# A GpSimd drain moved into the program's last tenth, two expert widths cut, and the last expert's tiles kept in order

## The chip, the cores and the metric

The kernel runs on one core of one Trainium2 chip. The metric is the device time of one execution in microseconds (us), as the median of several runs. A profile of one execution gives the trace from which the rows below are taken; its times count from the first instruction (the span's start). The engines are PE (matrix multiply; PEld is its weight load), DVE (vector), ACT (scalar), POOL (GpSimd, which also issues the indirect DMAs) and SP (which issues the plain DMAs). POOLq and the like are an engine's own instructions that are not computing, such as drains and branches.

## The reference

A windowed attention (4 batches, 8 heads, 576 positions of 64) is followed by a gated layer and by a mixture of 8 experts. The change is in the last part, which takes 2304 tokens `x` of 512 numbers:

```python
    expert_idx = np.argmax(logits, axis=1)
    ...
    gate_w = probs[np.arange(N), expert_idx]
    out = np.zeros((N, D), dtype=np.float32)
    for e in range(E):
        mask = expert_idx == e
        ...
        h = np.maximum(x[mask] @ w1[e], 0.0)
        out[mask] = gate_w[mask, None] * (h @ w2[e])
```

`w1[e]` is 512 by 1024, `w2[e]` 1024 by 512. The inputs send 346, 339, 358, 323, 280, 270, 222 and 166 tokens to the experts, in the order in which the kernel takes them.

## The kernel before

Each fp32 operand is split into a high and a low part, and every product is three matmuls (high by high, low by high, high by low). The experts are taken in slots: the first is expert 0, the second the fuller of the experts that are known first, the rest are in falling order of their token counts, which the kernel sorts at run time. Slot `e` has a static width, `CAPS[e]` (line 34): so many token columns are computed, and rows beyond the tokens that are there are not stored. Tokens beyond the width go to a loop behind the last expert (`tc.For_i`, line 1142), which runs as often as there are tiles left over; with the counts above it runs zero times, before and after the change.

The loop over the experts (lines 1091 to 1104) does for slot `e`:

- the gathers of the next expert's tokens, one indirect DMA on POOL for each tile of up to 128 rows (`gather`, line 928, tile `xg`), and the loads and splits of its weights (`weights`: 8 loads of 512 KB on SP, ACT's cast to `weh` at line 98, DVE's subtraction to `wel` at line 114);
- `ffn1`: eight groups `h0` to `h7`, each 12 matmuls (4 k-steps of 3) as wide as `CAPS[e]` (line 967), into one of two PSUM buffers; each group is evicted by ACT (relu, line 969) and then DVE (line 970);
- for each tile of the next expert the transposes `tx` (4 on PE, line 947), and for each own tile `ffn2`: 24 matmuls of 512 columns into `z` (line 983), DVE's scaling to `y` (line 987) and one indirect store on POOL (line 988). Each store to `out` waits for the landing of the one before.

These are the names of the code. In the rows the sixth expert is slot 5, the seventh slot 6 and the last slot 7; `h_2` is group 2, `xg_1`, `tx_1`, `y_1` and `z_1` belong to the second tile.

The order on each engine is not the code's: a scheduler that works on the whole program merges the steps. It issues z matmuls between h groups where it expects PE to wait. Each engine executes its own list in order. The code can pin an instruction with `tc.keep_in_program_order`, or tie what is inside a block behind an instruction with `tc.issue_after`; `latest(ENG.PE)[0]` is the last PE instruction written so far.

After the loop the program ends with a barrier: a drain on every engine (line 1203), on POOL three.

Of the kernel before, what the change touches and what calls it, by code (L numbers as in the profile page):

```python
# [1 line left out]

# [1 line left out]

# [21 lines left out]
E = 8  # L26
# [4 lines left out]
KD = DM // P  # L31
KF = FF // P
KE = FE // P
CAPS = [384, 384, 384, 352, 320, 320, 288, 256]
TCOL = NBLK
MAXOV = 16
BIG = 2.0 ** 42
# [21 lines left out]
def attn_ffn_moe(ctx: ExitStack, tc: tile.TileContext, qd, kd, vd, wgv, w_out, emb, tau, w1, w2, cst, ids, out):  # L59
    nc = tc.nc  # L60
# [13 lines left out]
    def pt(tag, name, bufs):  # L74
        return ps.tile([P, 512], F32, tag=tag, name=name, bufs=bufs)

    def row(name):
        return mid.tile([P, DM + 1], F32, tag="r", name=name)
# [487 lines left out]
    ENG = mybir.EngineType  # L566

    def latest(*engines):
        traced = nc.cur_bb.bb.instructions
        return [next(i for i in reversed(traced) if i.engine == e) for e in engines]  # L570
# [354 lines left out]
    def gather(e, t, idx, upto=None, w=P):  # L925
        x = row(f"xg{e}_{t}")
        if upto is None:
            nc.gpsimd.indirect_dma_start(out=x[0:w, :], out_offset=None, in_=x2_d, in_offset=IOA(ap=idx[0:w], axis=0))
        else:
            nc.gpsimd.memset(x, 0.0)  # L930
            nc.gpsimd.indirect_dma_start(out=x, out_offset=None, in_=x2_d[0:upto, :], in_offset=IOA(ap=idx, axis=0),
                                         bounds_check=upto - 1, oob_is_err=False)
        xg[e, t] = x
# [6 lines left out]
    def make_x(e, n, early=False):  # L940
        xe[e] = tuple(wide([P, KD, n], f"xe{z}_{e}", early) for z in range(2))

    def transp(e, t, u, w=P):
        xh, xl = xe[e]
        q = pt("t", f"tx{e}_{t}", 2)
        for k in range(KD):
            nc.tensor.transpose(q[:, k * P:k * P + w], xg[e, t][0:w, k * P:(k + 1) * P], ident[0:w, 0:w])
        qv = q.rearrange("p (k t) -> p k t", k=KD)[:, :, 0:w]
        sl = slice(u * P, u * P + w)
        hi_copy("a", xh[:, :, sl], qv)  # L950
        lo_sub("v", xl[:, :, sl], qv, xh[:, :, sl])

    def ffn1(e, n, early=False):
        xh, xl = xe.pop(e)
        hs = ([], [])
        for f in range(KE):
            if f % 4 == 0:
                for z in range(2):
                    hs[z].append(wide([P, 4, n], f"h{z}_{e}_{f}", early))
            hh, hl = (h[f // 4][:, f % 4, :] for h in hs)  # L960
            m = pt("s", f"h{e}_{f}", 2)
            cnt = 0
            fs = slice(f * P, (f + 1) * P)
            for k in range(KD):
                wh, wl = wset[e][k]
                for w, x in ((wh, xh), (wh, xl), (wl, xh)):
                    nc.tensor.matmul(m[:, :n], w[:, fs], x[:, k, :], start=(cnt == 0), stop=(cnt == 3 * KD - 1))  # L967
                    cnt += 1
            nc.scalar.activation(out=hh, in_=m[:, :n], func=AF.Relu)  # L969
            nc.vector.scalar_tensor_tensor(out=hl, in0=m[:, :n], scalar=0.0, in1=hh.bitcast(F32), op0=ALU.max,  # L970
                                           op1=ALU.subtract)
        return hs

    def ffn2(e, t, u, hs, idx, w=P):
        m = pt("m", f"z{e}_{t}", 3)
        cnt = 0
        ts = slice(u * P, u * P + w)
        for k in range(KE):
            hh, hl = (h[k // 4][:, k % 4, ts] for h in hs)
            wh, wl = wset[e][KD + k // 2]  # L980
            ds = slice((k % 2) * DM, (k % 2 + 1) * DM)
            for h, ww in ((hh, wh), (hl, wh), (hh, wl)):
                nc.tensor.matmul(m[0:w, :], h, ww[:, ds], start=(cnt == 0), stop=(cnt == 3 * KE - 1))  # L983
                cnt += 1
        x = xg.pop((e, t))
        y = row(f"y{e}_{t}")[:, 0:DM]
        nc.vector.tensor_scalar_mul(y[0:w, :], m[0:w, :], x[0:w, DM:DM + 1])  # L987
        nc.gpsimd.indirect_dma_start(out=out, out_offset=IOA(ap=idx[0:w], axis=0), in_=y[0:w, :], in_offset=None,  # L988
                                     bounds_check=NT - 1, oob_is_err=False)

    def ffn1_tok(e, t):
        xh, xl = xe.pop(e)
        hr = op_.tile([P, FE], F32, tag="c", name=f"hr{e}_{t}")
        hs = [op_.tile([P, KE, P], F32R, tag="c", name=f"hk{y}_{e}_{t}") for y in range(2)]
        for z in range(2):
            m = pt("s", f"ht{e}_{t}_{z}", 2)
            ds = slice(z * 512, (z + 1) * 512)
            cnt = 0
            for k in range(KD):
                wh, wl = wset[e][k]  # L1000
                for x, w in ((xh, wh), (xl, wh), (xh, wl)):
                    nc.tensor.matmul(m, x[:, k, :], w[:, ds], start=(cnt == 0), stop=(cnt == 3 * KD - 1))
                    cnt += 1
            nc.scalar.activation(out=hr[:, ds], in_=m, func=AF.Relu)
        for z in range(2):
            q = pt("t", f"th{e}_{t}_{z}", 2)
            for k in range(4):
                nc.tensor.transpose(q[:, k * P:(k + 1) * P], hr[:, (4 * z + k) * P:(4 * z + k + 1) * P], ident)
            qv = q.rearrange("p (k t) -> p k t", k=4)
            hi_copy("a", hs[0][:, 4 * z:4 * z + 4, :], qv)  # L1010
            lo_sub("v", hs[1][:, 4 * z:4 * z + 4, :], qv, hs[0][:, 4 * z:4 * z + 4, :])
        return [[h[:, 4 * z:4 * z + 4, :] for z in range(2)] for h in hs]
# [25 lines left out]
    def weights(e):  # L1038
        for j in range(NP):
            split_we(e, j, load_we(order[e], j, e), "a", "v")  # L1040

    hs = ffn1(0, CE * P)
# [8 lines left out]
    def load_col(e):  # L1051
        t0 = EARLY[e] if e < len(EARLY) else 0
        nt = -(-CAPS[e] // P) - t0
        cols[e] = cp.tile([P, nt], I32, tag=f"cols{e}", name=f"cols{e}")
        nc.sync.dma_start(cols[e], tab_v[:, bass.ds(order[e] * TCOL + t0, nt)])

    def col(e, t):
        t -= EARLY[e] if e < len(EARLY) else 0
        return cols[e][:, t:t + 1]
# [5 lines left out]
    def width(e, t):  # L1065
        return min(P, CAPS[e] - t * P)

    def tiles(e):
        return range(-(-CAPS[e] // P))

# [14 lines left out]
    transp(0, CE, 0)  # L1085
    make_x(1, CAPS[1] - P)
    for t in tiles(1)[1:]:
        transp(1, t, t - 1, width(1, t))
    hs = ffn1_tok(0, CE)
    ffn2(0, CE, 0, hs, col(0, CE))  # L1090
    for e in range(1, E):
        if e + 1 < E:
            for t in tiles(e + 1):
                gather(e + 1, t, col(e + 1, t), w=width(e + 1, t))
            weights(e + 1)
        t0 = EARLY[e] if e < len(EARLY) else 0
        hs = ffn1(e, CAPS[e] - t0 * P)
        if e + 1 < E:
            make_x(e + 1, CAPS[e + 1])
        for t in tiles(e):  # L1100
            if e + 1 < E and t in tiles(e + 1):
                transp(e + 1, t, t, width(e + 1, t))
            if t >= t0:
                ffn2(e, t, t - t0, hs, col(e, t), width(e, t))

    pn, pe, pb, po = small("pn", E), small("pe", E), small("pb", E), small("po", E)
    pi, cu = small("pi", E, I32), small("cu", E)
# [34 lines left out]
    with tc.For_i(0, nov, 1) as i:  # L1142
# [10 lines left out]
        hs = ffn1_tok(X, 0)  # L1153
# [53 lines left out]
```

## Time and profile before

| what | us |
|---|---|
| median of 3 runs | 918.26 (918.13 to 920.56) |
| the profiled execution | 916.44 |
| its span, first to last instruction | 914.4 |
| busy: PE, DVE, ACT, POOL | 874.6, 546.6, 437.9, 240.3 |
| sixth, seventh, last expert, and behind the last matmul | 31.99, 30.28, 22.41, 11.15 |

The span is from the first to the last instruction of the core; the execution's time has 2.04 us around it. Busy times are sums over the span, and engines work beside each other. The stages are cut at the first h matmul of an expert. The mean granted clock of TensorE is 0.977 of full speed.

### The profile page before, as it was taken

What the parts mean: (1) busy time and instruction counts of PE and PEld (TensorE: products, weight loads), DVE (VectorE), ACT (ScalarE), POOL (GpSimd) and SP (SyncE); (2) the same over time, 40 slices, a digit from 0 to 9 for tenths busy, and PEclk for the clock granted to TensorE, in tenths of its full rate; (3) what the DMA queues carried; (4) which work ended last, traced back from release to release, by engine and by line L of the source; (5) the groups of instructions that cost most, each with busy time, mean ns of one, the idle gap of its engine ahead of it and who ended that gap; (6) DMA issues with size and microseconds to landing.
All of it is one profiled execution on the core that took longest, in us unless ns stands there. A gap on an engine that the chain in (4) does not pass through costs nothing. (4 is left out here: it accounts for less than half of the span.)

```text
span 914.4 us, 14453 instructions
## 1 busy us (share of the span) xinstructions
PE 874.6 (96%) x5080; PEld 750.2 (82%) x5080; DVE 546.6 (60%) x1352; ACT 437.9 (48%) x943; POOL 240.3 (26%) x305
## 2 busy tenths in 40 slices
PE   6888999899999999999999999999999999999995
PEld 3578989899888888888878888888878989888874
DVE  4988967878888755564205554443855545445442
ACT  5666746676666663342215554443534334333330
POOL 2265624455655530000000000022130221230220
PEclk9788999999999999999999999999999999999998
DMA  7745434334333222483114345514356544553500
GB/s 205 267 145 184 148 106 127 101 117 131 109 122 128 90 96 84 150 273 115 47 47 116 116 139 137 160 50 128 98 169 206 198 158 157 173 191 126 170 25 15
DMA packets 69738, 121.69 MB, mean 133 GB/s; under 512 B 8280, under 2 KB 37080, under 8 KB 69666
## 3 DMA queue, kind: packets, MB, share of 16 engines
q1 hardware_dynamic: 65666, 110.53, 38.1%
q0 software_dynamic: 4000, 10.25, 3.4%
q8 instruction: 40, 0.66, 0.3%
q14 instruction: 32, 0.26, 0.1%
HBM read 97.06 MB, written 24.47 MB: 133 GB/s over the span
## 5 line engine op out<-in xcount | busy, mean ns | idle before, releaser
L482 PE MATMUL m<-x,wh 128*128 128x256 f32 (+1 forms) x1152 | 289.5, 342 | 0.0
L482 PEld LDWEIGHTS m<-x,wh 128*128 128x128 f32 x1152 | 198.2, 193 | 21.1 <-issue 0.5
L482 PE MATMUL m<-x,wl 128*128 128x256 f32 (+1 forms) x576 | 195.4, 339 | 0.0
L794 PE MATMUL y<-wo,gh 128*128 128x512 f32 x432 | 141.3, 401 | 0.0
L482 PEld LDWEIGHTS m<-x,wl 128*128 128x128 f32 x576 | 110.6, 192 | 11.4
L967 PE MATMUL h<-xe,weh 128*128 128x256 f32 (+4 forms) x512 | 107.6, 302 | 1.3 <-DVE lg L829 1.0
L983 PE MATMUL z<-weh,h 128*128 128x512 f32 (+3 forms) x336 | 106.6, 396 | 0.0
L794 PEld LDWEIGHTS y<-wo,gh 128*128 128x128 f32 x432 | 80.0, 188 | 17.4
L114 DVE TENSOR_TENSOR wel<-wer,weh 128x1024 fp32r<-128x1024 f32 x64 | 78.2, 1222 | 18.5 <-ACT weh L98 16.5
L967 PEld LDWEIGHTS h<-xe,weh 128*128 128x128 f32 x512 | 84.6, 188 | 4.1 <-DVE h L970 1.3
L794 PE MATMUL y<-wo,gl 128*128 128x512 f32 x216 | 86.0, 398 | 0.0
L967 PE MATMUL h<-xe,wel 128*128 128x256 f32 (+4 forms) x256 | 77.1, 301 | 0.0
L969 ACT ACTIVATE h<-h 128x256 fp32r<-128x256 f32 (+4 forms) x64 | 27.2, 425 | 95.6 <-PE h L967 94.4
L988 POOL DMA_INDIRECT out<-y,cols x20 | 26.5, 1324 | 172.6 <-DVE y L987 159.1
L983 PEld LDWEIGHTS z<-weh,h 128*128 128x128 f32 (+3 forms) x336 | 58.3, 178 | 15.2
L98 ACT CAST weh<-wer 128x1024 fp32r<-128x1024 f32 x64 | 66.1, 1044 | 6.1 <-DMA wer<-in_w 6.0
L881 POOL DMA_INDIRECT tab_d<-ids_sb,ai x18 | 18.3, 1016 | 186.4 <-DVE ai L878 169.8
L983 PE MATMUL z<-wel,h 128*128 128x512 f32 (+3 forms) x168 | 65.8, 392 | 0.0
L496 DVE SCALAR_TENSOR_TENSOR sg<-sg,m 128x512 f32<-128x512 f32 x54 | 36.8, 681 | 47.1 <-PE m L482 32.8
L250 ACT ACTIVATE p<-p,mx 128x256 f32<-128x256 f32 x112 | 55.3, 494 | 13.5 <-DVE mx L247 12.5
L492 ACT ACTIVATE sg<-m 128x512 f32<-128x512 f32 x54 | 32.1, 594 | 61.0 <-PE m L482 60.3
L810 ACT ACTIVATE xr<-y 128x512 f32<-128x512 f32 x18 | 10.8, 598 | 93.5 <-PE y L794 93.5
(212 smaller groups left out, 1555.1 us busy)
## 6 DMA issues: line engine op xcount, KB each, us to landing
wer<-in_w SPq DMA_DIRECT2D x64, 512.0 KB, 4.7
gT_d<-sg SPq DMA_DIRECT2D x54, 256.0 KB, 2.4
gl<-gT_d SPq DMA_DIRECT2D x27, 512.0 KB, 6.2
wr<-in_wgv SPq DMA_DIRECT2D x24, 512.0 KB, 6.1
kr<-in_kd SPq DMA_DIRECT2D x24, 320.0 KB, 3.1
qr<-in_qd SPq DMA_DIRECT2D x24, 256.0 KB, 2.7
wor<-in_w_out SPq DMA_DIRECT2D x12, 512.0 KB, 4.0
x_d<-xr SPq DMA_DIRECT2D x18, 256.5 KB, 4.7
```

Source lines behind the costliest of these rows:

```text
L98: nc.scalar.copy(o, i)
L114: e.tensor_tensor(out=o, in0=i, in1=h.bitcast(F32), op=ALU.subtract)
L250: nc.scalar.activation(out=p_t[:, j, f:], in_=p_t[:, j, f:], func=AF.Exp, scale=-1.0, bias=mx[:, j:j + 1], accum_out=su[:, j:j + 1])
L482: nc.tensor.matmul(m[:, z * n:(z + 1) * n], w[:, gv, k, :], x[k], start=(cnt == 0), stop=(cnt == 3 * KD - 1))
L492: nc.scalar.activation(out=sg[:, 0:512], in_=m, func=AF.Tanh, scale=0.5)
L496: nc.vector.scalar_tensor_tensor(out=sg[:, 0:512], in0=sg[:, 0:512], scalar=1.0, in1=m, op0=ALU.add, op1=ALU.mult)
L794: nc.tensor.matmul(m, g[:, k % 4, u * P:(u + 1) * P], w[:, k % 3, :], start=(k == 0 and z == 0), stop=(k == KF - 1 and z == 2))
L881: nc.gpsimd.indirect_dma_start(out=tab_d, out_offset=IOA(ap=ai[:, u:u + 1], axis=0), in_=ids_sb[:, t:t + 1], in_offset=None)
L967: nc.tensor.matmul(m[:, :n], w[:, fs], x[:, k, :], start=(cnt == 0), stop=(cnt == 3 * KD - 1))
L969: nc.scalar.activation(out=hh, in_=m[:, :n], func=AF.Relu)
L983: nc.tensor.matmul(m[0:w, :], h, ww[:, ds], start=(cnt == 0), stop=(cnt == 3 * KE - 1))
L988: nc.gpsimd.indirect_dma_start(out=out, out_offset=IOA(ap=idx[0:w], axis=0), in_=y[0:w, :], in_offset=None, bounds_check=NT - 1, oob_is_er ...
```

## The change

Three edits. The widths of slots 5 and 6 go from 320 and 288 to 288 and 256; slot 6 then has two tiles instead of three, and the third tile of slot 5 has 32 rows instead of 64. A drain is issued on GpSimd at the top of the last expert's pass through the loop and is kept in program order. The second layer (`ffn2`) of the last expert is tied behind the last PE instruction that stands ahead of it in the code, for each tile.

```diff
-from contextlib import ExitStack
+from contextlib import ExitStack, nullcontext
...
-CAPS = [384, 384, 384, 352, 320, 320, 288, 256]
+CAPS = [384, 384, 384, 352, 320, 288, 256, 256]
...
     for e in range(1, E):
+        if e + 1 == E:
+            tc.keep_in_program_order(nc.gpsimd.drain())
         if e + 1 < E:
...
             if t >= t0:
-                ffn2(e, t, t - t0, hs, col(e, t), width(e, t))
+                with tc.issue_after(latest(ENG.PE)[0]) if e + 1 == E else nullcontext():
+                    ffn2(e, t, t - t0, hs, col(e, t), width(e, t))
```

On PE, in the sixth expert behind group `h_1`, this stood before (the left name is written, the others are read):

```order
L967 MATMUL h_1_8701<-xe_5_8517,wel_3_8366 128x320
L947 MATMUL tx_0_8810<-cs,xg_0_8630 128x128 x4
L983 MATMUL z_0_8817<-weh_4_8371,h_5_0_8684 128x512
L967 MATMUL h_2_8716<-xe_5_8517,weh_0_8347 128x320
L967 MATMUL h_2_8716<-xe_5_8518,weh_0_8347 128x320
```

and this stands there now:

```order
L967 MATMUL h_1_8699<-xe_5_8517,wel_3_8366 128x288
L947 MATMUL tx_0_8808<-cs,xg_0_8630 128x128 x4
L983 MATMUL z_0_8815<-weh_4_8371,h_5_0_8682 128x512
L947 MATMUL tx_1_8845<-cs,xg_1_8632 128x128 x2
L967 MATMUL h_2_8714<-xe_5_8517,weh_0_8347 128x288
```

Two of the four transposes of the seventh expert's second tile moved here from behind the eighth h group; the other two stay there.

On PE, in the last expert behind group `h_1`, this stood before:

```order
L967 MATMUL h_1_9220<-xe_7_9098,weh_3_8945 128x256
L967 MATMUL h_1_9220<-xe_7_9097,wel_3_8946 128x256
L983 MATMUL z_0_9327<-weh_4_8951,h_7_0_9203 128x512
L983 MATMUL z_1_9357<-weh_4_8951,h_7_0_9203 128x512
L967 MATMUL h_2_9235<-xe_7_9097,weh_0_8927 128x256
```

and this stands there now, behind six matmuls of `h_0` and six of `h_1`:

```order
L967 MATMUL h_0_9167<-xe_7_9088,weh_2_8930 128x256
L967 MATMUL h_0_9167<-xe_7_9089,weh_2_8930 128x256
L967 MATMUL h_1_9182<-xe_7_9088,weh_2_8930 128x256
L967 MATMUL h_1_9182<-xe_7_9089,weh_2_8930 128x256
L967 MATMUL h_0_9167<-xe_7_9088,wel_2_8931 128x256
L967 MATMUL h_1_9182<-xe_7_9088,wel_2_8931 128x256
...
L967 MATMUL h_0_9167<-xe_7_9088,wel_3_8937 128x256
L967 MATMUL h_1_9182<-xe_7_9088,wel_3_8937 128x256
L967 MATMUL h_2_9197<-xe_7_9088,weh_0_8918 128x256
```

The first two groups are now mixed, k-step by k-step, and the three z matmuls that stood among the h groups (the third was behind `h_4`) are behind `h_7`.

On DVE, around the end of the seventh expert, this stood before:

```order
L114 TENSOR_TENSOR wel_2_8940<-wer_2_8937,weh_2_8939 128x1024
L987 TENSOR_SCALAR y_1_9168<-z_1_9143,xg_1_8632 128x512
L114 TENSOR_TENSOR wel_3_8946<-wer_3_8943,weh_3_8945 128x1024
L987 TENSOR_SCALAR y_2_9198<-z_2_9173,xg_2_8634 32x512
L114 TENSOR_TENSOR wel_4_8952<-wer_4_8949,weh_4_8951 128x1024
L970 SCALAR_TENSOR_TENSOR h_7_0_9204<-h_0_9205,h_7_0_9203 128x256
```

and this stands there now:

```order
L114 TENSOR_TENSOR wel_1_8925<-wer_1_8922,weh_1_8924 128x1024
L987 TENSOR_SCALAR y_1_9159<-z_1_9134,xg_1_8632 128x512
L114 TENSOR_TENSOR wel_2_8931<-wer_2_8928,weh_2_8930 128x1024
L114 TENSOR_TENSOR wel_3_8937<-wer_3_8934,weh_3_8936 128x1024
L970 SCALAR_TENSOR_TENSOR h_7_0_9166<-h_0_9167,h_7_0_9165 128x256
L970 SCALAR_TENSOR_TENSOR h_7_0_9166<-h_1_9182,h_7_0_9165 128x256
```

The splits `wel_2` and `wel_3` of the last expert's weights now stand behind the y of the seventh's last tile; `wel_4` moved behind the evictions of `h_0` and `h_1`. On POOL the gather and the store of the seventh's third tile are gone, and the drain stands behind the store of its second tile and ahead of the first store of the last expert.

## Rows read from the trace of the kernel before

**Rows 1.** Stages: busy us (instructions) of PE, PEld, DVE, ACT, POOL; clock, DMA share, GB/s.

```profile
818.57:850.56 31.99, 31.99 (x182) 27.38 (x180) 16.23 (x21) 11.41 (x18) 6.92 (x6) 1.00 0.44 153
850.56:880.84 30.28, 30.28 (x177) 25.15 (x176) 15.30 (x20) 10.96 (x17) 5.15 (x3) 1.00 0.33 118
880.84:903.25 22.41, 22.35 (x145) 19.75 (x143) 9.43 (x14) 5.89 (x11) 2.62 (x2) 1.00 0.03 12
```

**Rows 2.** PE in order of time: start us, us, line, operation, count.

```profile
818.57 0.46 PE L967 MATMUL h<-xe,weh 128*128 128x320 f32 x2
...
822.10 0.60 PE L947 MATMUL tx<-cs,xg 128*128 128x128 f32 x4
822.45 0.47 PE L983 MATMUL z<-weh,h 128*128 128x512 f32 x1
...
858.03 0.42 PE L967 MATMUL h<-xe,weh 128*128 128x288 f32 x2
...
861.21 0.63 PE L983 MATMUL z<-weh,h 128*128 128x512 f32 x2
...
875.28 0.62 PE L983 MATMUL z<-weh,h 128*32 128x512 f32 x2
...
880.84 0.39 PE L967 MATMUL h<-xe,weh 128*128 128x256 f32 x2
...
883.56 0.62 PE L983 MATMUL z<-weh,h 128*128 128x512 f32 x2
884.03 0.40 PE L967 MATMUL h<-xe,weh 128*128 128x256 f32 x2
...
888.12 0.39 PE L983 MATMUL z<-weh,h 128*128 128x512 f32 x1
...
902.85 0.40 PE L983 MATMUL z<-wel,h 128*128 128x512 f32 x1
```

**Rows 3.** DVE in order of time, in brackets the idle time before and its releaser.

```profile
875.48 0.75 DVE L987 TENSOR_SCALAR y<-z,xg 128x512 f32<-128x512 f32 x1 [2.40 <-PE z L983]
876.15 1.21 DVE L114 TENSOR_TENSOR wel<-wer,weh 128x1024 fp32r<-128x1024 f32 x1
...
884.18 0.43 DVE L970 SCALAR_TENSOR_TENSOR h<-h,h 128x256 fp32r<-128x256 f32 x1 [0.94 <-ACT h L969]
...
903.29 0.75 DVE L987 TENSOR_SCALAR y<-z,xg 128x512 f32<-128x512 f32 x1 [4.29 <-PE z L983]
```

**Rows 4.** POOL in order of time, same columns.

```profile
816.88 0.96 POOL L928 DMA_INDIRECT xg<-x_d,cols  x1 [0.31 <-issue]
...
899.28 0.98 POOL L988 DMA_INDIRECT out<-y,cols  x1 [15.59 <-DVE y L987]
904.32 0.98 POOL L988 DMA_INDIRECT out<-y,cols  x1 [4.06 <-DVEq L1142]
```

**Rows 5.** The last store of y, the DMA's landing.

```profile
DMA to landing us min/median/max: 2.5/2.5/2.5
```

**Rows 6.** Line 1203 by engine: count, min/median/max ns, first and last start.

```profile
L1203 POOLq DRAIN  x3: 46/103/5302, 907.9 to 913.8; - x3
...
L1203 DVEq DRAIN  x2: 10/14/17, 908.1 to 913.5; - x2
```

**Rows 7.** The gather issued at 816.88, its landing.

```profile
DMA to landing us min/median/max: 6.7/6.7/6.7
```

**Rows 8.** Line 1195, the program's start, same columns.

```profile
L1195 POOLq DRAIN  x1: 189/189/189, 0.3 to 0.3; - x1
```

**Rows 9.** DMA queues of the page: packets, MB, share of 16 engines.

```profile
q0 software_dynamic: 4000, 10.25, 3.4%
```

**Rows 10.** PE in order of time, in the attention part.

```profile
168.25 0.33 PE L307 MATMUL o<-pl,vs 128*128 128x128 f32 x1 [1.47 <-DVE pl L114]
```

**Rows 11.** Busy time in two stretches, columns as in rows 1.

```profile
168.50:171.90 3.40, 3.40 (x18) 3.40 (x18) 2.28 (x12) 2.89 (x10) 0.73 (x2) 0.50 0.36 127
318.00:322.00 4.00, 3.02 (x22) 2.52 (x21) 1.42 (x3) 0.74 (x2) 1.17 (x1) 1.00 0.16 62
```

## The prediction

> **What bounds the kernel now.** The page gives the span, 914.4 us; the busy time by stage shows what fills its last tenth [rows 1]. The three stretches are the sixth, the seventh and the last expert: in each the matmul engine (PE) is busy for all but 0.06 us, while DVE, ACT and POOL are busy for between a tenth and a half of it. So in these stages time is worth what PE's instructions take, plus any gap that opens between them. PE's instructions in order of time [rows 2] give the rates, from start to start: 24 matmuls of 320 columns in 822.10 - 818.57 = 3.53 us (0.1471 each), 24 of 288 in 861.21 - 858.03 = 3.18 us (0.1325), 36 of 256 in 888.12 - 884.03 = 4.09 us (0.1136); a tile of 24 matmuls of 512 columns with 32 rows takes 880.84 - 875.28 = 5.56 us, four transposes 822.45 - 822.10 = 0.35 us.
>
> PE's last matmul starts at 902.85 [rows 2]. Behind it stands a chain without PE: DVE's scaling of y from 903.29 for 0.75 us [rows 3], POOL's store from 904.32 [rows 4], which lands 2.5 us after its issue [rows 5], at 906.8, then POOL's drains [rows 6]: of the three of line 1203 the first, at 907.9, takes 5302 ns, which is to 913.2; the others take 46 and 103 ns. The span ends 1.2 us later, so the long one stands in it in full.
>
> **The sixth expert (288 for 320).** Its 96 matmuls of line 967 become 96 x (0.1325 - 0.1471) = -1.40 us. Its own third tile keeps its 24 matmuls of line 983 (with 32 rows they take 5.56/24 = 0.232 each, and two of full height at 883.56 take 0.235 each: rows save no time), so narrower there is nothing. The four transposes of the seventh's third tile, which stood in this stage, are gone: -0.35.
>
> One moved step costs. The first two transposes of the seventh's second tile now stand behind 24 h matmuls, 4 transposes and one z matmul; before they stood behind all eight h groups. PE gets there at 818.57 + 24 x 0.1325 + 0.35 + 0.23 (the z matmul) = 822.33. The gather that fills their input is issued by POOL at 816.88 [rows 4] and lands 6.7 us later [rows 7], at 823.58; nothing ahead of it in POOL's order changes. PE executes in order, so all of h2 to h7 stands behind this wait: +1.25. If that gather landed as early as the last store does (2.5 us), the wait would be 0. Sum of the stage: -1.40 - 0.35 + 1.25 = -0.50 (bounds -1.75 and -0.50).
>
> **The seventh expert (256 for 288).** 96 x (0.1136 - 0.1325) = -1.81, and its third tile goes: -5.56. Its y, its gather and its store, on DVE and POOL, were hidden behind PE and give nothing. Its h matmuls come in groups of 12 x 0.1136 = 1.36 us; a group's eviction, through ACT and DVE, ends 884.18 + 0.43 - 883.56 = 1.05 us after the next matmul's start [rows 2, 3], and with two PSUM buffers a group waits only for the one before the last, so evictions keep pace. I put 0.2 for small gaps (bounds 0 and 0.4): -7.17.
>
> **The last expert, kept in order.** Its own matmuls stay: 96 x 0.1136 + 48 x 0.232 = 22.03 of the stage's 22.41 us [rows 1], so 0.38 us were gaps and the last matmul's tail. Three things now stand otherwise. (a) The two splits wel 2 and wel 3 stand on DVE behind y of the seventh's second tile, which waits for the matmul that ends just where this stage starts; before, that place was the third tile's, and 5.56 us of its matmuls covered them. From the trace: that y starts 0.20 us after the tile's end (875.48 - 875.28), a wel starts at 876.15 and takes 1.21 [rows 3], so wel 2 is there 2.08 us after the stage's start and wel 3 at 3.29. PE, whose first groups are now interleaved so that h0 and h1 take each k-step in turn, wants wel 2 after 16 matmuls, at 1.82 (wait 0.26), and wel 3 six matmuls later, at 2.08 + 0.68 = 2.76 (wait 0.53). (b) h0 ends one matmul before h1, and no z matmul is left to fill: h2 waits for h0's eviction, 1.05 - 0.11 = 0.94 us. (c) Behind that, the evictions come 1.05 us after groups of 1.36 us, with wel splits of 1.21 us between; where such a split stands ahead of an eviction (h5's) up to 0.44 us may be late, and I take 0. Sum: 0.26 + 0.53 + 0.94 - 0.21 (the gaps of before: 0.38 less 0.17 for the last matmul's tail, 0.40 - 0.23) = +1.52 (bounds +0.6 and +2.2). z of the last tile is still the last work, so the chain of y and store behind it is unchanged.
>
> PE's end therefore moves by -0.50 - 7.17 + 1.52 = -6.15, say **-6.1 us**.
>
> **The drain.** A GpSimd drain is added between the last store of the seventh expert and the first of the last one. It holds no wait of its own; behind it in POOL's order stand only the two stores. POOL sits idle for 15.59 us ahead of the first of them [rows 4], so 5.3 us there are hidden; they would be paid only if y of the first last-expert tile came within 5.3 us. What it does to the final drain no row shows directly. From below: nothing, the final one stays at 5.30 us. From above: it goes to the length of a drain with no DMA since the last one, 0.05 to 0.19 us (the 46, 103 and 189 ns rows [rows 6, 8]). The long one is the only one that stands behind DMAs that POOL issued: the software queue moved 4000 packets [rows 9]; the 189 ns one stands before the first, and the two short ones have none since the drain ahead of them. If the 5.1 us above 0.19 go with these packets, 256 of them (the last two stores, 128 rows each) leave 0.33, and the final drain is 0.5 us: **-4.8**. I take this value, since the three short rows differ from the long one in exactly that.
>
> The Trainium skill ("VectorE: DVE Perf Modes", section "The DRAIN you can't avoid") says that the drains of the pre- and postamble are about 12 ns, constant, on all five engines. The row of DVE agrees (10 to 17 ns), POOL's 5302 ns does not; by the rule there would be nothing for the added drain to take over, and the time would be that of rival (1).
>
> **Sum.** -6.1 - 4.8 = -10.9: span 903.5, the profiled execution 916.44 - 10.9 = 905.5. The median of the runs, 918.26, stands 1.82 above the profiled execution, so **907.3 us**.
>
> **Rivals.** (1) The final drain stays at 5.30 us, because its length is that of its place (the end of the program, with the branches of the loop just left) and not of the DMAs ahead. For it: no row shows a drain shortened by another; the other short rows are drains at places of their own. Then only -6.1: 912.1 us. Half a drain (a fixed part if any DMA came since) lies between, near 909.7. (2) The gaps cost clock. PE gets two gaps of about 1 us, ahead of the two transposes and ahead of h2 of the last expert. Once in the trace a gap of 1.47 us, before 168.25 [rows 10], was followed by 3.40 us at a granted clock of 0.50, which is the 1.2 GHz level; the stretch from 318 to 322, of whose 4.00 us PE is busy for 3.02, was granted 1.00 [rows 11]. A stretch at half clock costs half its length: 1.7 us for the like of that one, 909.0 us. To come out slower than before it would have to hold at 1.2 GHz for more than 21.8 us (10.9 lost), that is for the whole of the last expert: 22.41 us at half speed cost 22.4 more, about 930 us. Against it: no gap of about 1 us in these rows did it, and PE is busy right up to both gaps. (3) The transposes' wait is hidden or the gather is earlier, and the last expert's evictions keep up better: 1.25 + 0.5 less, 905.5 us. (4) The evictions of the last expert are all late, because an in-order DVE puts a split of 1.21 us ahead of one in three: +1.5, 908.8 us.
>
> **Chances.** Forecast with (3) and (4), the drain short: 0.64. Drain unchanged 0.22, half 0.06. Clock lost for a short stretch 0.05, for most of the last expert 0.03. A measurement of this kernel can tell about 0.3%, 2.8 us, from no change: a case is within it if less than 2.8 us are won, which wants the drain unchanged and over 3.5 us of new gaps, 0.05 of the whole. So faster 0.91, same 0.05, slower 0.04. The range has the forecast with its own bounds below (905.0) and rival (1) with its stage bounds above (913.5).
>
> **What would show it.** Right: POOL has a drain of about 5 us near 875 to 881 and one under 1 us at the end; PE waits about 1.2 us for a gather behind the first z of the sixth expert, and about 0.9 us ahead of h2 of the last; the seventh expert's stage falls from 30.3 to about 23.1 us; the last one's grows from 22.4 to about 23.9. Wrong: a final drain of 5.3 us (step on the drain), a granted clock under 1.0 between 816 and 897, or a last stage over 25 us.

## The result, and the profile after

The changed kernel takes 909.15 us (median of 4 runs, 905.75 to 910.52) against 919.41 us (918.13 to 920.81) for the kernel before in the same set of runs: a ratio of 0.9886, 95% interval 0.9857 to 0.9916. The prediction was 907.3 us, with a range of 905.0 to 913.5. The profiled execution took 905.75 us, the shortest of the four; its span is 903.6.

The stages of the changed kernel, cut as in [rows 1] (columns as there), and the stretch behind them:

```profile
818.81:849.64 30.83, 30.46 (x177) 25.11 (x176) 15.40 (x20) 10.01 (x16) 7.10 (x5) 1.00 0.46 159
849.64:872.91 23.27, 23.20 (x154) 20.79 (x152) 12.13 (x17) 10.73 (x17) 2.26 (x2) 1.00 0.43 145
872.91:897.51 24.60, 23.19 (x145) 20.07 (x143) 11.80 (x16) 6.71 (x12) 2.71 (x2) 1.00 0.05 19
897.51:903.60 6.09, 0.00 (x1) 0.00 (x0) 0.75 (x1) 0.00 (x0) 0.98 (x1) 0.66 0.04 13
```

Against [rows 1] the sixth expert went from 31.99 to 30.83 us, the seventh from 30.28 to 23.27, the last from 22.41 to 24.60, and what stands behind the last matmul from 11.15 to 6.09. That is -1.16, -7.01, +2.19 and -5.06, together -11.0; the sixth expert starts 0.24 later, which leaves the 10.8 us by which the span fell. The clock was granted in full in all three stages.

POOL's drains, by line (the added one, and those of the program's end; durations in ns, then the first and last start):

```profile
L1093 POOLq DRAIN  x1: 6932/6932/6932, 873.9 to 873.9; - x1
```

```profile
L1206 POOLq DRAIN  x3: 52/103/220, 902.3 to 903.3; - x3
```

POOL's stores around the added drain, in order of time, with the idle time before each in brackets:

```profile
874.13 1.72 POOL L988 DMA_INDIRECT out<-y,cols  x1 [4.93 <-DVE y L987]
893.08 0.99 POOL L988 DMA_INDIRECT out<-y,cols  x1 [17.22 <-DVE y L987]
898.58 0.98 POOL L988 DMA_INDIRECT out<-y,cols  x1 [4.50 <-DVEq L1145]
```

The added drain's record begins at 873.9, ahead of the store at 874.13 that stands in front of it, so its 6.93 us hold that store's issue too. It ends at 880.83; from the end of the issue (875.85) that is 4.98 us. The next store comes at 893.08, so nothing waited for it. At the program's end the drain of 5302 ns [rows 6] is now 220 ns; the other two take 103 and 52 ns (103 and 46 before).

PE in the sixth expert, then in the last one, in order of time:

```profile
822.34 0.47 PE L983 MATMUL z<-weh,h 128*128 128x512 f32 x1
823.19 0.41 PE L947 MATMUL tx<-cs,xg 128*128 128x128 f32 x2 [0.37 <-DMA xg<-x_d,cols]
823.35 0.51 PE L967 MATMUL h<-xe,weh 128*128 128x288 f32 x2
...
874.28 0.62 PE L967 MATMUL h<-xe,weh 128*128 128x256 f32 x4
875.04 0.50 PE L967 MATMUL h<-xe,wel 128*128 128x256 f32 x2
875.38 0.63 PE L967 MATMUL h<-xe,weh 128*128 128x256 f32 x4
876.18 0.50 PE L967 MATMUL h<-xe,wel 128*128 128x256 f32 x2 [0.17 <-DVE wel L114]
877.50 0.50 PE L967 MATMUL h<-xe,weh 128*128 128x256 f32 x2 [0.82 <-DVE h L970]
...
884.31 0.28 PE L967 MATMUL h<-xe,wel 128*128 128x256 f32 x1
884.87 0.50 PE L967 MATMUL h<-xe,weh 128*128 128x256 f32 x2 [0.28 <-DVE h L970]
```

The z matmul at 822.34 takes 0.23, so the transposes at 823.19 waited 0.62 for their gather. In the last expert four matmuls take 0.45: PE waited 0.31 ahead of 875.04 (wel 2), 0.35 ahead of 876.18 (wel 3), 1.32 - 0.23 = 1.09 ahead of h2 at 877.50, and 0.56 - 0.11 = 0.45 ahead of h7 at 884.87 (60 matmuls, which are h2 to h6, stand between the two).

What PE waited for, on DVE: wel 2 and wel 3 behind y of the seventh's last tile, then the evictions of h0 and h1; further on a split, and h5's eviction right behind it:

```profile
873.11 0.75 DVE L987 TENSOR_SCALAR y<-z,xg 128x512 f32<-128x512 f32 x1 [2.72 <-PE z L983]
873.77 2.35 DVE L114 TENSOR_TENSOR wel<-wer,weh 128x1024 fp32r<-128x1024 f32 x2
877.02 0.76 DVE L970 SCALAR_TENSOR_TENSOR h<-h,h 128x256 fp32r<-128x256 f32 x2 [0.89 <-ACT h L969]
...
883.26 1.23 DVE L114 TENSOR_TENSOR wel<-wer,weh 128x1024 fp32r<-128x1024 f32 x1 [0.51 <-ACT weh L98]
884.40 0.42 DVE L970 SCALAR_TENSOR_TENSOR h<-h,h 128x256 fp32r<-128x256 f32 x1
```

Behind each wait the second matmul comes late too: from 875.04 to 875.38 there are two matmuls in 0.34 us, where a stream of them takes 0.23. So of the 1.09 ahead of h2, 0.11 belongs to the wait for wel 3.

### The profile page after: what moved, and what is told of

It is laid out like the page before. It is cut to its first block, busy times and chain, and to the rows that moved or that the text cites. A ratio compares the mean times of both kernels' runs of the same rounds, so it can differ in the third digit from the quotient of the medians.

```text
span 903.6 us, 14387 instructions
## 1 busy us (share of the span) xinstructions
PE 866.4 (96%) x5052; PEld 743.6 (82%) x5052; DVE 545.7 (60%) x1350; ACT 436.8 (48%) x942; POOL 237.6 (26%) x303
## 3 DMA queue, kind: packets, MB, share of 16 engines
q0 software_dynamic: 3904, 10.12, 3.5%
## 5 line engine op out<-in xcount | busy, mean ns | idle before, releaser
L482 PEld LDWEIGHTS m<-x,wl 128*128 128x128 f32 x576 | 110.4, 192 | 11.5
L983 PE MATMUL z<-weh,h 128*128 128x512 f32 (+3 forms) x320 | 101.8, 396 | 0.0
L983 PEld LDWEIGHTS z<-weh,h 128*128 128x128 f32 (+3 forms) x320 | 56.4, 180 | 14.1
L983 PE MATMUL z<-wel,h 128*128 128x512 f32 (+3 forms) x160 | 62.9, 393 | 0.0
L810 ACT ACTIVATE xr<-y 128x512 f32<-128x512 f32 x18 | 10.8, 597 | 93.5 <-PE y L794 93.5
## 6 DMA issues: line engine op xcount, KB each, us to landing
wr<-in_wgv SPq DMA_DIRECT2D x24, 512.0 KB, 10.8
```

What stands on the lines that cost most here:

```text
L482: nc.tensor.matmul(m[:, z * n:(z + 1) * n], w[:, gv, k, :], x[k], start=(cnt == 0), stop=(cnt == 3 * KD - 1))
```

## The experiments

The profiles differ by up to 4.4 us before the changed part is reached (the sixth expert starts between 818.38 and 822.76; the changed kernel itself has 818.81 in one run and 821.15 in another), though nothing ahead of it was changed but the drains of e4 and, with the new widths, the sixth expert's third tile (its gather and transposes have 32 rows for 64); most of the spread is there by PE's 1500th matmul (226.7 to 230.6 us). So the parts are compared from that start on. A stage is then from the first h matmul of its expert to the next one's, the last one up to the start of the last matmul; before, that is 31.99, 30.28 and 902.85 - 880.84 = 22.01 us [rows 2], with 914.4 - 902.85 = 11.5 us behind. The runs of the kernel before in these sets had medians of 919.78 (e1 to e4) and 920.08 us (e5 to e8); e9 and e10 were run on another chip, where the kernel before took 916.47 us in its one run. A single execution of the kernel before took between 916.22 and 921.3 us, so where there is one run the stages of its trace are the evidence, not its time.

### The drain alone (e1)

The added drain, with the widths and the order of before:

```diff
...
     for e in range(1, E):
+        if e + 1 == E:
+            tc.keep_in_program_order(nc.gpsimd.drain())
```

> Only the added GpSimd drain, widths and order of before. Theory (the drain's time is a backlog of the indirect DMAs that POOL issued since the last drain): the added drain takes about 5 us inside POOL's idle time ahead of the last expert's first store, the final one falls from 5.30 to 0.2 to 0.5 us, PE's last matmul stays where it was; 5.1 us less than before, about 913 us. Rival (the length belongs to the place at the program's end): the final drain stays at 5.3 us and the time at 918 us.

914.3 us, ratio 0.9948 (0.9928 to 0.9967). The stages stayed at 31.98, 30.28 and 22.17 us; behind the last matmul 6.49 us instead of 11.5. POOL's drains:

```profile
L1093 POOLq DRAIN  x1: 7004/7004/7004, 884.2 to 884.2; - x1
```

```profile
L1205 POOLq DRAIN  x3: 52/103/220, 910.4 to 911.2; - x3
```

The final drain fell to 220 ns with the number of DMAs of before and the program's end as it was. Its length is not that of its place: rival (1) of the prediction falls. From the sixth expert's start the kernel took 90.93 us against 95.80, 4.9 less.

### The change without the drain (e2)

```diff
-        if e + 1 == E:
-            tc.keep_in_program_order(nc.gpsimd.drain())
```

> The changed kernel without the added drain. Theory: PE ends as in the changed kernel (897.1 us), the final drain is back at 5.0 to 5.3 us, so about 5 us longer than the changed kernel, near 914 us. Rival (the final drain is short for another reason, such as the two DMAs fewer or the new order): final drain 0.2 us, time as the changed kernel, 909 us.

912.74 us, ratio 0.993 (0.9906 to 0.9953). The final drain:

```profile
L1204 POOLq DRAIN  x3: 46/103/5138, 904.8 to 910.5; - x3
```

It is back, and with 62 DMAs since the program's start instead of 64 it is 0.164 us shorter than before. Behind the last matmul stand 11.2 us; the seventh and the last stage are those of the change (23.25 and 24.20 us). The sixth took 31.67: there the gather of the moved transposes landed 6.9 us after its issue, against 6.0 in the run above. By the medians the step from here to the change is 3.6 us (912.74 to 909.15); from the sixth expert's start it is 90.32 - 84.76 = 5.6, of which 0.8 is that gather.

### The change without the tie (e3)

The z matmuls of the last expert are free again:

```diff
-                with tc.issue_after(latest(ENG.PE)[0]) if e + 1 == E else nullcontext():
-                    ffn2(e, t, t - t0, hs, col(e, t), width(e, t))
+                ffn2(e, t, t - t0, hs, col(e, t), width(e, t))
```

> The changed kernel with the last expert's z matmuls free again (four of them then stand between h3 and h4, others further on). Theory: the mixed h0 and h1, the late wel 2 and wel 3 and the wait before h2 come from the width (the third tile that is gone), not from the tie, and stay; the wait of 0.45 us before h6 may go or be filled, so the last stage is 24.1 to 24.6 us instead of 24.60 and the time 0 to 0.5 us less than the changed kernel. Rival (the tie makes the gaps): last stage 22.4 to 23 us, 1.6 to 2.2 us less.

909.87 us, ratio 0.9906 (0.9876 to 0.9936). The last stage took 24.35 us (24.21 with the tie); the waits ahead of wel 2, wel 3 and h2 are as long without the tie as with it, 0.31, 0.35 and 1.09 us. The wait that the expectation puts ahead of h6 is h7's; z matmuls fill most of it here, and the stage is no shorter for it. What I had not expected stands behind it: 8.34 us from the last matmul to the end, against 6.46 with the tie. DVE's two last y and POOL's two stores in order of time:

```profile
896.52 0.75 DVE L987 TENSOR_SCALAR y<-z,xg 128x512 f32<-128x512 f32 x1 [4.83 <-PE z L983]
898.14 0.75 DVE L987 TENSOR_SCALAR y<-z,xg 128x512 f32<-128x512 f32 x1 [0.88 <-PE z L983]
...
897.54 0.99 POOL L988 DMA_INDIRECT out<-y,cols  x1 [21.22 <-DVE y L987]
901.06 0.98 POOL L988 DMA_INDIRECT out<-y,cols  x1 [2.52 <-DMA out<-y,cols]
```

Free, the matmuls of the two z tiles mix, and the two y come 1.6 us apart; with the tie they come 5.50 apart (892.05 and 897.55). Stores to `out` wait for the landing of the one before, and POOL stood idle for 2.52 us here until that landing; with the change's 1.03 us from y to store it would have started 1.9 us earlier. This is what the tie is worth: 8.34 - 6.46 = 1.9 us behind the last matmul, and 0.14 in the stage. The medians, 909.87 and 909.15 us, can't tell the two apart; e10 shows the same wait a second time.

### A drain in every pass (e4)

```diff
-        if e + 1 == E:
-            tc.keep_in_program_order(nc.gpsimd.drain())
+        tc.keep_in_program_order(nc.gpsimd.drain())
```

> The changed kernel with a drain at the top of every expert's pass, seven in all. Theory (backlog of about 0.08 us for each indirect DMA): the first takes about 2 us, each later one (5 to 6 DMAs since the last) 0.4 to 0.6 us from the end of the POOL instruction ahead of it, the final one 0.2 us; gathers start that much later, time within 1 us of the changed kernel. Rival (a fixed length once any DMA came): each takes about 5 us, the gathers behind them are late by as much, PE waits for them and the time is 3 us or more longer. Second rival (the clock time or the size moved since the last drain counts): lengths that do not follow the count.

907.97 us in one run. The seven drains, and the final ones:

```profile
L1092 POOLq DRAIN  x7: 3714/4827/6927, 697.7 to 876.0; - x7
```

```profile
L1205 POOLq DRAIN  x3: 52/103/215, 904.5 to 905.8; - x3
```

The figures expected for the seven were wrong. Each stands right behind a store, with 30, 5, 6, 6, 6, 5 and 2 DMAs since the drain ahead, and none ended before that store had landed (3.4 to 6.4 us from the start of its issue). So a drain also waits for a DMA that is under way. Behind the landing, taken from the trace to the nanosecond, the seven took:

| DMAs since the drain ahead | from the store's landing to the drain's end, us |
|---|---|
| 30 | 1.280 |
| 6 | 0.282, 0.282, 0.283 |
| 5 | 0.247, 0.241 |
| 2 | 0.119 |

This goes by number as well: (1.280 - 0.119) / 28 = 0.041 us for each DMA. The seven cost PE little: of the 1.5 us more than in the change from the sixth expert's start to the end (86.26 us) 1.0 is in the sixth's stage (31.82), where the gather of the moved transposes was issued 1.79 us ahead of the stage, as in the change (1.80), but landed later (7.0 us from its issue); 0.2 is in the seventh's and 0.3 behind the last matmul.

Drains with nothing under way show the number by itself. All final drains of these kernels stand behind a store that has landed, where the trace has its landing (the 64 DMAs of before are 23 gathers, 23 stores and 18 writes of the routing table):

| DMAs of POOL since the drain ahead | final drain, us | kernel |
|---|---|---|
| 64 | 5.302 | before, e5 |
| 62 | 5.138 | e2, e10 |
| 2 | 0.220 | after, e1, e3, e6 to e8 (e4: 0.215) |
| 1 | 0.138 | e9 |

From 1 DMA to 64 that is (5.302 - 0.138) / 63 = 0.082 us for each DMA and 0.056 us by itself; 62 and 2 lie on this line (5.140 and 0.220). Drains with no DMA since the one ahead took 0.046 to 0.103 us, and 0.189 at the program's start. The early drains fit too, counted from the end of the store's issue: 4.98 us for 60 in the change, 5.14 for 62 (e1), 5.06 for 61 (e9). Their stores landed 1.0 to 1.8 us after the issue's end, well ahead of half of that time. With the 0.041 us of the seven, which is half of 0.082, the reading that fits all of them is that half of a drain's price goes by while it waits for the landing and half stands behind it; no run shows the inside of a drain.

### The tie alone (e5)

Widths and drain as before, z of the last expert tied as in the change:

```diff
...
             if t >= t0:
-                ffn2(e, t, t - t0, hs, col(e, t), width(e, t))
+                with tc.issue_after(latest(ENG.PE)[0]) if e + 1 == E else nullcontext():
+                    ffn2(e, t, t - t0, hs, col(e, t), width(e, t))
```

> Only the tie of the last expert's z matmuls, widths and drain as before. Theory (the waits in the last expert come from the third tile that is gone): h0 and h1 stand one behind the other as before, h2 does not wait, only the 0.2 us around 888 grows by the one z matmul that filled it: last stage 22.4 to 22.8 us, final drain 5.3 us, span within 0.5 us of before from the sixth expert's start. Rival (my prediction: keeping order makes the waits): last stage 23.9 us or more, with about 0.9 us ahead of h2.

917.97 us in one run; the last stage took 22.21 us (22.01 before), the final drain 5302 ns. PE at the start of that stage, at h2's place 24 matmuls later, and at its only wait:

```profile
882.20 0.39 PE L967 MATMUL h<-xe,weh 128*128 128x256 f32 x2
...
884.92 0.39 PE L967 MATMUL h<-xe,weh 128*128 128x256 f32 x2
...
889.45 0.50 PE L967 MATMUL h<-xe,weh 128*128 128x256 f32 x2 [0.29 <-DVE h L970]
```

24 matmuls of 0.1134 end at 882.20 + 2.72 = 884.92, where h2 starts without a wait. The tie does not make the waits of the change; it lengthens the wait at h5, where a z matmul stood before, and the stage by 0.2 us.

### The last y behind the splits (e6)

In the change, y of the seventh's second tile is tied behind wel 3 of the last expert on DVE (`welo` holds the instruction):

```diff
-        nc.vector.tensor_scalar_mul(y[0:w, :], m[0:w, :], x[0:w, DM:DM + 1])
+        with tc.issue_after(welo[e + 1, 3]) if (e, t) == (6, 1) else nullcontext():
+            nc.vector.tensor_scalar_mul(y[0:w, :], m[0:w, :], x[0:w, DM:DM + 1])
```

> The changed kernel with the seventh expert's last y tied behind wel 2 and wel 3 of the last expert on DVE. Both theories expect the waits for wel 2 (0.31) and wel 3 (0.35) gone. Theory that the wait before h2 comes from mixing h0 with h1 by itself: it stays at 1.0 to 1.1 us, last stage 24.60 - 0.66 = 23.9 us. Rival (h2 waits only because the splits were late): its wait falls too, last stage under 23.2 us.

908.19 us in one run. PE in the last expert's first two groups:

```profile
877.79 0.62 PE L969 MATMUL h<-xe,weh 128*128 128x256 f32 x4
878.24 0.39 PE L969 MATMUL h<-xe,wel 128*128 128x256 f32 x2
878.47 0.62 PE L969 MATMUL h<-xe,weh 128*128 128x256 f32 x4
878.92 0.39 PE L969 MATMUL h<-xe,wel 128*128 128x256 f32 x2
880.13 0.50 PE L969 MATMUL h<-xe,weh 128*128 128x256 f32 x2 [0.82 <-DVE h L972]
```

Four matmuls take 0.45 and nothing waits for wel 2 or wel 3 any more, but h2 at 880.13 still waits 1.21 - 0.23 = 0.98 us, for DVE's eviction of h0: as long as in the change, whose 1.09 holds the 0.11 behind the wait for wel 3. The last stage took 23.32 us to the last matmul, 0.89 less than the change's 24.21. The splits and the mix of h0 with h1 each have their own wait.

### Three ties (e7), and the change once more (e8)

To e6 two ties on PE are added: h1 of the last expert behind h0, and the transposes of the seventh's second tile behind the sixth's first z tile.

```diff
+                    with tc.issue_after(end0) if (e, f) == (E - 1, 1) else nullcontext():
-                    nc.tensor.matmul(m[:, :n], w[:, fs], x[:, k, :], start=(cnt == 0), stop=(cnt == 3 * KD - 1))
+                        nc.tensor.matmul(m[:, :n], w[:, fs], x[:, k, :], start=(cnt == 0), stop=(cnt == 3 * KD - 1))
...
+            if f == 0:
+                end0 = latest(ENG.PE)[0]
...
-                transp(e + 1, t, t, width(e + 1, t))
+                with tc.issue_after(latest(ENG.PE)[0]) if (e, t) == (5, 1) else nullcontext():
+                    transp(e + 1, t, t, width(e + 1, t))
```

> The changed kernel with three ties: the seventh's last y behind wel 2 and wel 3 on DVE, the last expert's h1 behind h0 on PE, the transposes of the seventh's second tile behind the sixth's first z tile. Theory: the waits for the gather (0.62), for the two splits (0.66) and before h2 (1.09) go: sixth stage 30.83 - 0.62 = 30.2, last stage 24.60 - 1.75 = 22.85 us, in all 2.4 us less than the changed kernel from the sixth expert's start. Rival (the waits only move, to h3, to the evictions behind y on DVE, or to the transposes' eviction): less than 1 us.

> The changed kernel once more, beside the version with three ties on the same chip. All theories: stages of 30.8, 23.3 and 24.6 us, final drain 0.22 us, 9 to 11 us under the kernel before.

e7: 907.88 us, ratio 0.9874 (0.9846 to 0.9903); e8: 908.41 us, ratio 0.9881 (0.9846 to 0.9917). These two can't be told apart by their medians. Their traces can: from the sixth expert's start to the end e7 took 83.06 us, the change 84.80 in e8 (84.76 in its first profile), with the sixth and the last stage at 30.26 and 22.89 us against 30.84 and 24.19. The waits left on PE in e7:

```profile
882.01 0.28 PE L970 MATMUL h<-xe,wel 128*128 128x256 f32 x1
882.47 0.50 PE L970 MATMUL h<-xe,weh 128*128 128x256 f32 x2 [0.18 <-DVE h L975]
...
886.57 0.28 PE L970 MATMUL h<-xe,wel 128*128 128x256 f32 x1
887.13 0.50 PE L970 MATMUL h<-xe,weh 128*128 128x256 f32 x2 [0.29 <-DVE h L975]
```

They are 0.46 - 0.11 = 0.35 us ahead of h4 and 0.56 - 0.11 = 0.45 ahead of h7, each for an eviction (of h2 and of h5) that stands behind a split of 1.23 us on DVE. With h1 behind h0 the wait ahead of h2 is gone, though no z matmul fills its place: it was the mix that made it. 1.7 us were won of 2.4 forecast: the wait ahead of h4 is new, and the seventh stage is 0.15 us longer (23.45 against 23.30). The wait ahead of h7 stayed, and the forecast had not counted on it.

### The drain one store later (e9)

```diff
+        if (e, t) == (E - 1, 1):
+            tc.keep_in_program_order(nc.gpsimd.drain())
         nc.gpsimd.indirect_dma_start(out=out, out_offset=IOA(ap=idx[0:w], axis=0), in_=y[0:w, :], in_offset=None,
```

(and the one at the top of the loop is gone.)

> The changed kernel with the added drain moved one store later, between the two stores of the last expert. Theory (the drain takes about 0.083 us for each of the 61 DMAs since the start, counted from the end of the store ahead of it): it ends about 5.1 us behind that store's issue, some 0.5 us after y of the last tile is ready, so the last store starts about 0.5 us late, and the final drain is near 0.14 us; span end 6.9 us behind the last matmul instead of 6.5. Rival (a drain is only as long as its own wait for the store to land): it ends about 2.5 us after the store's issue and costs nothing.

906.23 us in one run. POOL's drains and the two last stores:

```profile
L989 POOLq DRAIN  x1: 6284/6284/6284, 892.0 to 892.0; - x1
...
L1206 POOLq DRAIN  x3: 52/103/138, 902.9 to 903.9; - x3
```

```profile
892.23 0.99 POOL L990 DMA_INDIRECT out<-y,cols  x1 [17.18 <-DVE y L987]
899.15 0.98 POOL L990 DMA_INDIRECT out<-y,cols  x1 [5.93 <-issue]
```

The drain ended at 898.28, which is 5.06 us behind the end of the store's issue; the store waited for nothing else and started 0.87 us later. With y of the last tile at 896.70 it would have started at 897.73 (y to store is 898.58 - 897.55 = 1.03 in the change), so it was 1.4 us late, and 7.89 us stand behind the last matmul instead of 6.46. The price of a drain is the same there; what changed is its cover. I had put 0.5 us, with the store at the drain's end.

### The widths alone (e10)

```diff
...
-CAPS = [384, 384, 384, 352, 320, 320, 288, 256]
+CAPS = [384, 384, 384, 352, 320, 288, 256, 256]
```

> Only the two widths, no tie and no drain. Theory: the mixed h0 and h1 and the wait of about 1.1 us ahead of h2 are there without the tie; last stage 24.2 to 24.4 us to the last matmul, the two last stores behind one another as without the tie (the last store waits for the landing of the one before), final drain 5.1 us: about 13 us from the last matmul to the end. Rival (my prediction: the tie makes the waits): last stage 22 to 23 us.

913.89 us in one run. PE in the last expert:

```profile
877.02 0.63 PE L967 MATMUL h<-xe,weh 128*128 128x256 f32 x4
877.81 0.50 PE L967 MATMUL h<-xe,wel 128*128 128x256 f32 x2 [0.16 <-DVE wel L114]
879.13 0.50 PE L967 MATMUL h<-xe,weh 128*128 128x256 f32 x2 [0.81 <-DVE h L970]
```

The mix, the late wel 3 and the wait ahead of h2 are there without a tie, and the last stage took 24.21 us. Behind it stand 13.10 us: a final drain of 5138 ns, and the last store at 902.11, for which POOL stood idle for 2.51 us until the one before had landed, as in e3.

## Why the prediction was right, point by point

- **The sixth expert: -0.50 forecast, -1.16 measured.** Rates and the transposes that went were right (e9, where nothing waits, took 30.27 us; 31.99 - 1.75 is 30.24); the wait behind the moved transposes was mis-sized. PE reached them at 822.57 and waited 0.62 us, not 1.25, since the gather landed 6.0 us after its issue at 817.01 instead of 6.7 [rows 7]. The same stage took 30.27 (e9), 30.84 (e8), 31.04 (e3), 31.33 (e10), 31.44 (e6) and 31.67 (e2) us in other runs of this order, with landings 5.2, 6.0, 6.2, 6.5, 6.7 and 6.9 us after the issue: the wait is real, and its size changes with the landing from run to run.
- **The seventh expert: -7.17 forecast, -7.01 measured.** As worked out; the small gaps came to 0.36 us, for 0.2.
- **The last expert: +1.52 forecast, +2.19 measured.** The waits (a) and (b) came out as 0.31, 0.35 and 1.09 us for 0.26, 0.53 and 0.94. Term (c), late evictions, I had taken as 0 with a bound of 0.44; it is 0.45: h5's eviction stands behind a split on DVE, and h7 waits for it. That is most of the 0.7 us that were missing. The rest is the 0.11 us by which the second matmul behind a wait comes late, for which the sum had no term.
- **What I put those waits down to was right in one part and wrong in the other.** (a) was put down to the third tile that is gone, and that holds: with it 5.56 us of cover go, and y then stands ahead of the splits; e3 and e10 have these waits without the tie. (b) was put down to the mix of h0 with h1 and to the z matmuls that no longer fill the place ahead of h2, under a heading that names the order kept by the tie. The mix holds, the tie does not: e5 has the tie and no wait there, e3 and e10 have the wait without the tie, and e7 has none with the tie kept and h1 behind h0. The scheduler makes the mix with the new widths alone (e10).
- **What the tie does I missed.** I wrote that the chain of y and store is unchanged. With the new widths it is unchanged only because of the tie: without it the last store waits for the landing of the other, POOL stands idle for 2.5 us (e3, e10), and the kernel ends 1.9 us later (e3).
- **The drain: -4.8 forecast, -5.08 measured.** The mechanism was right: the drain's time goes with the DMAs that POOL issued since the one before (e1, e2, and the tables at e4). The size was right to 0.3 us: it goes by DMAs (2 of 64), where I had counted packets (256 of 4000). The 256 were misread too: each of the two last stores moved 80 packets. By packets the table's steps would differ, 1.7 ns for each from 62 to 64 DMAs (3904 to 4000 packets) and 1.0 ns for each from 1 to 2 (80 packets); by DMAs both are 0.082 us. The drain's cover ahead of the last expert's first store held. The Trainium skill ("VectorE: DVE Perf Modes", section "The DRAIN you can't avoid") gives the drains of the pre- and postamble as about 12 ns, constant, on all five engines. Here the program's own drains agree on DVE (10 to 17 ns) and not on POOL (46 to 5302 ns).
- **The rivals.** The drain that stays where it is fell with e1. No stretch of the three stages was under full clock, though PE waited 1.09 us in one. Rivals (3) and (4) each came in by a part: 0.63 us of the gather's wait did not happen, and 0.45 us of late evictions did.
- **The sum.** -1.16 - 7.01 + 2.19 - 5.06 and 0.24 at the start give -10.8 of the span; -10.9 was forecast. That the misses of the sixth and of the last expert (-0.7 and +0.7) cancel is luck. The forecast of the median, 907.3, was 1.85 us short of 909.15 all the same: it set the runs 1.82 us above the profiled execution, as before, but this profiled execution stands 3.4 us below their median.
- **What each edit is worth.** From the sixth expert's start to the end the kernel before took 95.80 us, the widths alone 92.07 (e10), with the tie 90.32 (e2), with the drain 84.76. The gather's landing moves each of these by up to 0.8 us.

## What to carry to other kernels

In these runs a GpSimd drain at the program's end pays for every indirect DMA since the last drain; one placed earlier, where POOL is idle for longer than it takes, moves that time off the end, and it should stand where no store behind it can be late (e9). When a tile is cut away, look at what its matmuls covered: here 2.2 of 7.0 us came back as waits in the next stage. Two final stores that wait for each other's landing want their producers apart, not interleaved.

## What the runs showed of the hardware

- A GpSimd drain behind a landed store took 0.056 us and 0.082 us for each indirect DMA since the drain ahead (1, 2, 62 and 64 DMAs: 0.138, 0.220, 5.138 and 5.302 us).
- Behind a store that was under way it ended after the landing, by 0.119 us with 2 DMAs, 0.241 to 0.283 with 5 or 6 and 1.280 with 30 (e4): 0.041 us for each. With 60 DMAs it ended 3.34 us behind it (the change), 4.98 behind the issue.
- The landing of one and the same gather, issued 1.8 us ahead of the sixth expert each time, took 5.2 (e9) to 6.9 us (e2), which moved that stage between 30.27 and 31.67 us.
- Behind a wait of PE the second matmul of 256 columns started 0.22 us after the first, against 0.11 in a stream.
- Ahead of the sixth expert the runs differ by up to 4.4 us (818.38 to 822.76), and by 3.9 us at PE's 1500th matmul (226.7 to 230.6); the cause is open.
